# Two tiles ahead of the weights, and q and k in 512 B packets that PSUM copies put in order

## The chip, the cores and the metric

One core of a Trainium2 chip. The metric is the device time of one execution in microseconds (us), the median of several runs. A profile shows one such run. Its engines are PE (TensorE, matmuls), PEld (its weight loads), DVE (VectorE), ACT (ScalarE), POOL (GpSimd) and SP (SyncE, which only issues DMA here). "tile" below means 256 tokens: the kernel works through 12 of them.

## The reference, cut to what matters

```python
# q, k, v: (4, 8, 768, 64), 0.1 * normal; 3 of 8 heads attend to all earlier keys,
# the others to 4 first keys and a window of 64
scores = (q @ k.T) / 8, masked;  a = softmax(scores);  attn = a @ v
x = attn.transpose(0, 2, 1, 3).reshape(3072, 512)
h = x @ w_in            # 512 x 2048
out = (h - tanh(h)) @ w_out
```

## The kernel before

Each operation is given to a small planner with an engine, an expected duration and what it reads and writes. The planner runs a list schedule over these durations and emits every engine's instructions in the order that it found.

```python
# loads of one tile: 128 tokens to a transfer, one token of 256 B (64 fp32) to a packet
r = lazy(raw_pool, [128, NB, H, D], FP32, "raw", f"raw_{nm}{t}")
for i in range(NB):                                   # NB = 2
    op("SP", 420, lambda ...: nc.sync.dma_start(
        out=r()[:, i, :, :], in_=src[b, :, s0 : s0 + 128, :].rearrange("h p d -> p h d")), ...)
...
# st_T: q and k of a pair of heads are transposed by PE into PSUM, then copied to SBUF
tp, key = bank([128, 2, NB, 128], FP16, "sc", f"tp{n}")
...
cost = {"ACT": 373, "DVE": 288}                       # what the planner is told, in ns
op(eq, cost[eq], lambda: copy(eq, qT[n]()[:], tp()[:, 0, :, :].rearrange("p i c -> p (i c)")), ...)
for hh in range(2):                                   # the two heads of k
    op(ek[hh], cost[ek[hh]], lambda ...: copy(
        ek[hh], kk[p_, hh, cs], tp()[p_, 1, :, :].rearrange("p i c -> p (i c)")), ...)
...
# the opening: weights are issued before tile 1
cast_qk(0, ...); cast_v(0)
for j in range(4): load_w_in(j)
scale_v(0); load(1)
for n in range(HP): st_T(n, "ACT", ("DVE", "DVE")); ...
cast_qk(1, ...); cast_v(1); scale_v(1)
for j in range(4): load_w_out(j)
load(2)
```

After the opening each tile has an up-projection (H: 8 units of 8 matmuls), a tanh on ScalarE and one VectorE instruction per unit, and a down-projection (O), while the attention of the tile after next goes on between them: transposes, copies to qT and kz, scores (sc), exp on ScalarE, masks (pt), the product with v (av), normalisation (x) and a transpose back (xT).

The softmax here doesn't subtract the row's maximum and nothing guards it: scores larger than these inputs give would overflow.

Of the kernel before, what the change touches and what calls it, by code (L numbers as in the profile page):

```python
# [7 lines left out]
FP32 = mybir.dt.float32  # L8
# [8 lines left out]
class Plan:  # L17
# [14 lines left out]

    def op(self, eng, ns, fn, r=(), w=(), dma=None, prio=None):
        i = len(self.ops)
        deps = set()
        for k in r:
            if k in self.writer:
                deps.add(self.writer[k])
            self.readers.setdefault(k, []).append(i)
        for k in w:  # L40
            if k in self.writer:
                deps.add(self.writer[k])
            deps.update(self.readers.get(k, ()))
            self.writer[k] = i
            self.readers[k] = []
        for key in (*r, *w):
            if isinstance(key, tuple) and key[0] in self.bufs:
                tag, at = key[:2]
                deps.update(self.users.get((tag, at - self.bufs[tag]), ()))
                self.users.setdefault((tag, at), []).append(i)  # L50
        deps.discard(i)
        self.ops.append((eng, ns, fn, deps, dma, i if prio is None else prio))
        return i

    def run(self):
# [14 lines left out]
        order = []  # L70

        def enqueue(i):
            queue[self.ops[i][0]].append(i)

        def finish(i, done):
            self.done[i] = done
            e, ns, _, _, dma, _ = self.ops[i]
            for u in users[i]:
                to = self.ops[u][0]
                if to == e and e == "PE":  # L80
                    at = self.start[i] + ns
                else:
                    at = done + (60 if to == "PE" else 40)
                ready[u] = max(ready[u], at)
                left[u] -= 1
                if not left[u]:
                    enqueue(u)
# [4 lines left out]
        while len(order) < n:  # L92
            t, e = min(
                [(max(free[e], min(ready[i] for i in q)), e) for e, q in queue.items() if q],
                default=(1e12, None),
# [17 lines left out]
            elif nxt < t:  # L113
# [3 lines left out]
            i = min(  # L117
                (i for i in queue[e] if ready[i] <= t), key=lambda i: self.ops[i][5]
            )
            queue[e].remove(i)  # L120
            _, ns, _, _, dma, _ = self.ops[i]
            self.start[i] = t
            order.append(i)
            free[e] = t + max(ns - self.OVERLAP[e], 40)
            if dma:
                packets, each = dma
                rings["POOL" if e == "POOL" else "SP"].append(
                    [i, t + ns + 300, each, packets * each / 16]
                )
            else:  # L130
                finish(i, t + ns + self.RESULT[e])
# [6 lines left out]
def kernel(  # L138
# [85 lines left out]

    def load(t, names="qkv"):
        b, g = divmod(t, NG)
        for nm in names:
            src = {"q": q, "k": k, "v": v}[nm]
            idx = 3 * t + "qkv".index(nm)
            r = lazy(raw_pool, [128, NB, H, D], FP32, "raw", f"raw_{nm}{t}")  # L230
            for i in range(NB):
                s0 = g * TT + i * 128
                op(
                    "SP", 420,
                    lambda r=r, i=i, src=src, s0=s0: nc.sync.dma_start(
                        out=r()[:, i, :, :],
                        in_=src[b, :, s0 : s0 + 128, :].rearrange("h p d -> p h d"),
                    ),
                    w=[("raw", idx, i)], dma=(1024, 21.0),
                )  # L240
            raws[nm, t] = (r, idx)

    W_OUT_AFTER = 2
    w_in_t = []
    w_out_t = []

    def load_w_in(j):
        w = lazy(w_pool, [128, HP, 512], FP16, f"win{j}", f"win{j}")
# [5 lines left out]
            ),  # L254
            r=[("v1", 0, 0)], w=[("win", j)], dma=(512, 80.0),
        )
        w_in_t.append(w)

    def load_w_out(j):
        w = lazy(w_pool, [128, 4, DM], FP16, f"wout{j}", f"wout{j}")  # L260
# [5 lines left out]
            ),  # L266
            r=[("v1", 0, W_OUT_AFTER)], w=[("wout", j)], dma=(512, 80.0),
        )
# [10 lines left out]
    )  # L279
    load(0, "qk")  # L280
    load(0, "v")

# [79 lines left out]
    for h in range(H):  # L362
# [5 lines left out]
            ),  # L368
            r=["thr", "A4", "A40", "A41", "A43"], w=[("m4", h // 2)],
        )  # L370
# [13 lines left out]

    def cast_qk(t, engines):

        for nm, es in zip("qk", engines):
            c = lazy(t16_pool, [128, NB, H, D], FP16, f"t16{nm}", f"t16_{nm}{t}")
            r, slot = raws[nm, t]
            for i, e in enumerate(es):  # L390

                def fn(c=c, r=r, i=i, e=e):
                    if e == "ACT":
                        nc.scalar.copy(out=c()[:, i, :, :], in_=r()[:, i, :, :])
                    else:
                        engs[e].tensor_copy(out=c()[:, i, :, :], in_=r()[:, i, :, :])  # L396

                op(
                    e, {"ACT": 590, "DVE": 380, "POOL": 540}[e], fn,
                    r=[("raw", slot, i)], w=[("t16" + nm, t, i)],  # L400
                )
            t16s[nm, t] = c

    v1s = {}
    vfs = {}

    def cast_v(t):
        b, g = divmod(t, NG)
        if g == 0:
            v1s[b] = lazy(v_pool, [128, 2 * NG, H, D + 1], FP16, "v1", f"v1_{b}")  # L410
            vfs[b] = lazy(v_pool, [128, 4, H, D + 1], FP16, "vf", f"vf_{b}")
        v1, vf, lo = v1s[b], vfs[b], g * NB
        r, slot = raws["v", t]
        op(
            "POOL", 200,
            lambda: nc.gpsimd.memset(v1()[:, lo : lo + NB, :, D : D + 1], 1.0 / XS),
            w=[("v1", b, lo + i) for i in range(NB)],
        )
        for i in range(NB):
            op(  # L420
                "POOL", 540,
                lambda i=i: nc.gpsimd.tensor_copy(  # L422
                    out=v1()[:, lo + i, :, 0:D], in_=r()[:, i, :, :]
                ),
                r=[("raw", slot, i)], w=[("v1", b, lo + i)],
            )

    def scale_v(t):
        b, g = divmod(t, NG)
        v1, vf, lo = v1s[b], vfs[b], g * NB  # L430
        for jb in range(lo, min(lo + NB, 4)):
# [6 lines left out]
                ),  # L438
                r=[("v1", b, jb), "rflag0", "rflag"], w=[("vf", b, jb)],
            )  # L440
# [4 lines left out]
    x16s = {}  # L445
    xTs = {}

    def st_T(n, eq="DVE", ek=("DVE", "DVE")):
# [6 lines left out]
        def mm():  # L455
# [8 lines left out]
            "PE", 224, mm,  # L464
            r=["ident"] + [("t16" + nm, t, i) for nm in "qk" for i in range(NB)], w=[key],
        )
        qT[n] = lazy(qt_pool, [128, TT], FP16, f"qT{hp}", f"qT{n}")

        def copy(e, dst, src):
            if e == "ACT":  # L470
                nc.scalar.copy(out=dst, in_=src)  # L471
            else:
                nc.vector.tensor_copy(out=dst, in_=src)  # L473

# [3 lines left out]
            eq, cost[eq],  # L478
            lambda: copy(eq, qT[n]()[:], tp()[:, 0, :, :].rearrange("p i c -> p (i c)")),
            r=[key], w=[(f"qT{hp}", t)],  # L480
        )
        for hh in range(2):
# [3 lines left out]
                lambda p_=p_, hh=hh: copy(  # L486
                    ek[hh], kk[p_, hh, cs], tp()[p_, 1, :, :].rearrange("p i c -> p (i c)")
                ),
# [18 lines left out]
    def st_S(n, gi):  # L507
# [35 lines left out]
        if gi == 0:  # L543
# [14 lines left out]

            op("DVE", 560 if g == 0 else 695, mask, r=pk + [("m4", hp)], w=pk)

    avs = {}

    def st_A(n, i):
# [19 lines left out]
        r = [("pt", n, gi) for gi in range(len(GROUPS[g]))]  # L583
        r += [("v1", b, jb) for jb in range(max(qb - 1, 0), qb + 1)]
        r += [("vf", b, jb) for jb in range(qb - 1)]
# [18 lines left out]

    def st_X(n):
        t, hp = divmod(n, HP)
        if hp == 0:
            xTs[t] = lazy(xt_pool, [128, HP, TT], FP16, "xT", f"xT{t}")
        xp, key = bank([128, NB, 128], FP16, "m", f"xp{n}")

        def mm():
            for i in range(NB):
# [5 lines left out]
        op(  # L618
            "DVE", 290,
            lambda: nc.vector.tensor_copy(  # L620
                out=xTs[t]()[:, hp, :], in_=xp()[:].rearrange("p i c -> p (i c)")
            ),
            r=[key], w=[("xT", t, hp)],
# [102 lines left out]

    cast_qk(0, (("DVE", "DVE"), ("DVE", "ACT")))
    cast_v(0)
    for j in range(4):
        load_w_in(j)  # L730
    scale_v(0)
    load(1)
    for n in range(HP):
        st_T(n, "ACT", ("DVE", "DVE"))
        if n:
# [5 lines left out]
        if n > 2:  # L741
            st_X(n - 3)
    for f in scores(HP - 1):
        f()
    for n in (HP - 2, HP - 1):
        st_A(n, 0)
        st_A(n, 1)
        st_X(n - 1)
    st_X(HP - 1)
    cast_qk(1, (("DVE", "DVE"), ("DVE", "POOL")))  # L750
    cast_v(1)
    scale_v(1)
    for j in range(4):
        load_w_out(j)
    load(2)
    for hp in range(HP):
# [76 lines left out]
```

## Time and profile before

| | before |
|---|---|
| time, median of 3 (lowest to highest) | 276.85 us (276.75 to 277.22) |
| TensorE work, counted by matmul pitch | 235 us |
| VectorE busy | 179.6 us, 65% |
| copy from PSUM to kz on VectorE | 283 ns, 96 times |

### The profile page before, as it was taken

How to read it: one execution, taken by the hardware profiler on the slowest of the kernel's cores; microseconds unless marked ns; L12 is line 12 of the kernel's file. 1: busy time of each engine (PE TensorE's matmuls, PEld its weight loads, DVE VectorE, ACT ScalarE, POOL GpSimd, SP SyncE). 2: the span in 40 equal slices, each digit the busy share in tenths (PEclk: the TensorE clock that was granted, in tenths of full speed). 3: DMA queues.
4: the chain of work that ended last, by engine and by line, in shares of the span. 5: the costliest groups of instructions: out<-in, count | busy, mean ns of one | idle time of the engine just before them, and what ended most of it. 6: DMA issues, size and time to landing. Idle time of an engine off the chain costs nothing.

```text
span 275.6 us, 6251 instructions
## 1 busy us (share of the span) xinstructions
PE 251.2 (91%) x2560; PEld 186.9 (68%) x2560; DVE 179.6 (65%) x452; ACT 154.2 (56%) x223; POOL 69.5 (25%) x116
## 2 busy tenths in 40 slices
PE   0457977999999999999999999999999999999984
PEld 0335764888778777777777777777777877776631
DVE  7784775776898875556987655567987655554310
ACT  2330464788357676665476776564567566644420
POOL 7530940527190730206803000300300000000000
PEclk9999999999999999999999999999999999999999
DMA  7999999999989590182860210010001001011101
GB/s 140 217 199 209 191 207 203 221 220 232 230 177 201 129 224 32 40 190 66 201 144 15 76 43 4 37 40 38 2 38 40 2 38 40 1 40 39 40 38 76
DMA packets 82733, 29.78 MB, mean 108 GB/s; under 512 B 75536, under 2 KB 79632, under 8 KB 82704
## 3 DMA queue, kind: packets, MB, share of 16 engines
q1 hardware_dynamic: 78336, 25.17, 41.7%
q0 software_dynamic: 4224, 4.19, 9.2%
q8 instruction: 20, 0.33, 0.5%
q14 instruction: 9, 0.07, 0.1%
q10 hardware_dynamic: 144, 0.01, 0.0%
HBM read 27.27 MB, written 6.29 MB: 122 GB/s over the span
## 4 chain that ended last, share of the span: by engine, by line
PE 84%; DVE 11%; ACT 2%; issue 2%
PE ph L642 29%; PE po L678 29%; PE sc L522 13%; PE av L578 8%; PE tp L458 3%; PE xp L613 2%; DVE x L597 1%; DVE kz L473 1%; DVE gt L662 1%; DVE pt L554 1%; DVE pt L549 1%; DVE kz L331 1%; DVE m L365 1%; DVE xT L620 1%; ACT th L655 1%
## 5 line engine op out<-in xcount | busy, mean ns | idle before, releaser
L642 PE MATMUL ph<-xT,win 128*128 128x256 f16 x768 | 103.3, 278 | 0.7 <-DVE gt L662 0.7
L678 PE MATMUL po<-wout,gt 128*128 128x512 f16 x384 | 100.0, 379 | 1.4 <-ACT ot L691 1.4
L537 ACT ACTIVATE pt<-sc 128x1024 f16<-128x1024 f32 (+1 forms) x96 | 85.5, 916 | 23.7 <-PE sc L522 19.4
L655 ACT ACTIVATE th<-ph 128x512 f32<-128x512 f32 x96 | 57.4, 598 | 71.4 <-PE ph L642 67.5
L662 DVE SCALAR_TENSOR_TENSOR gt<-th,ph 128x512 f16<-128x512 f32 x96 | 65.8, 686 | 38.6 <-ACT th L655 38.1
L642 PEld LDWEIGHTS <-win 128*128 128x128 f16 x768 | 73.8, 100 | 16.3 <-issue 1.1
L522 PE MATMUL sc<-qT,kz 128*128 128x128 f16 (+1 forms) x448 | 53.2, 250 | 2.5 <-DVE kz L473 2.0
L678 PEld LDWEIGHTS <-gt 128*128 128x128 f16 x384 | 34.2, 98 | 23.3 <-issue 1.9
L522 PEld LDWEIGHTS <-kz 128*128 128x128 f16 x448 | 37.0, 99 | 14.1 <-DVE kz L473 2.8
L578 PEld LDWEIGHTS <-pt 128*128 128x128 f16 x672 | 30.1, 98 | 9.6 <-issue 2.1
L396 POOL CAST t_q<-raw_q 128x512 f16<-128x512 f32 x20 | 12.4, 646 | 90.3 <-PE tp L458 47.5
L578 PE MATMUL av<-v,pt 128*128 128x65 f16 x352 | 29.3, 196 | 1.5 <-DVE xT L620 0.8
L473 DVE COPY kz<-tp 64x256 f16<-64x256 f16 x96 | 27.1, 283 | 3.4 <-ACT qT L471 1.2
L554 DVE TENSOR_TENSOR pt<-pt,m 128x1024 f16<-128x1024 f16 x32 | 23.3, 729 | 4.7 <-ACT pt L537 4.7
L578 PE MATMUL av<-vf,pt 128*128 128x65 f16 x320 | 23.5, 193 | 1.6 <-DVE xT L620 0.9
L458 PE MATMUL tp<-ident,t_q 128*128 128x128 f16 x96 | 13.8, 226 | 9.2 <-DVE t_q L396 8.8
L691 ACT ACTIVATE ot<-po 128x512 f32<-128x512 f32 x24 | 14.4, 598 | 12.9 <-PE po L678 12.7
L597 DVE TENSOR_TENSOR x<-av,rinv 128x256 f16<-128x256 f32 x48 | 20.3, 423 | 1.5
L592 DVE RECIPROCAL rinv<-av 128x4 f32<-128x4 f32 x48 | 8.7, 180 | 17.7 <-PE av L578 17.2
L422 POOL CAST v<-raw_v 128x512 f16<-128x512 f32 x24 | 15.0, 641 | 18.7 <-DMA raw_v<-in_v_dram 18.5
L435 POOL TENSOR_TENSOR vf<-v,rflag 128x520 f16<-128x520 f16 x16 | 18.2, 1146 | 0.7
L458 PEld LDWEIGHTS <-t_q 128*128 128x128 f16 x96 | 8.8, 101 | 13.4 <-DVE t_q L396 8.9
(35 smaller groups left out, 121.7 us busy)
## 6 DMA issues: line engine op xcount, KB each, us to landing
raw_q<-in_q_dram SPq DMA_DIRECT2D x24, 256.0 KB, 4.9
raw_k<-in_k_dram SPq DMA_DIRECT2D x24, 256.0 KB, 4.8
raw_v<-in_v_dram SPq DMA_DIRECT2D x24, 256.0 KB, 4.9
out_dram<-ot SPq DMA_DIRECT2D x24, 256.0 KB, 2.1
win<-in_moe_w_in_dram POOLq DMA_DIRECT2D x4, 512.0 KB, 10.4
wout<-in_moe_w_out_dram POOLq DMA_DIRECT2D x4, 512.0 KB, 10.6
retr_i<-in_is_retrieval_dram ACTq DMA_DIRECT2D x1, 8.0 KB, 3.1
```

The costliest lines, as they stand in the source:

```text
L435: lambda jb=jb, fl=fl: nc.gpsimd.tensor_mul(out=vf()[:, jb, :, :], in0=v1()[:, jb, :, :], in1=fl[:].unsqueeze(2).to_broadcast([128, H, D + ...
L458: nc.tensor.transpose(out=tp()[:, x, i, :], in_=c()[:, i, 2 * hp : 2 * hp + 2, :], identity=ident16[:],)
L473: nc.vector.tensor_copy(out=dst, in_=src)
L522: nc.tensor.matmul(out=sc()[:, hh, o : o + nb * 128], lhsT=kk[:, hh, jb * 128 : jb * 128 + 128], rhs=qT[n]()[:, q0 * 128 : (q0 + nb) * 128 ...
L537: lambda: nc.scalar.activation(out=pt()[:, :, 512 * gi : 512 * gi + wid], in_=sc()[:, :, 0:wid], func=AF.Exp, scale=inv_sqrt_d,),
L554: nc.vector.tensor_mul(out=pv, in0=pv, in1=m4[:, hs, 256:512].unsqueeze(2).to_broadcast([128, 2, 2, 256]),)
L578: nc.tensor.matmul(out=av()[:, i, hh, :], lhsT=pt()[:, hh, co : co + 128], rhs=vv()[:, jb, h, :], start=(jb == 0), stop=(jb == qb),)
L597: lambda: nc.vector.tensor_mul(out=x16()[:], in0=av()[:, :, :, 0:D], in1=rinv()[:].unsqueeze(3).to_broadcast([128, NB, 2, D]),),
L642: nc.tensor.matmul(out=ph()[:, j, :], lhsT=w_in_t[fb // 4]()[:, cb, f0 : f0 + 128], rhs=xTs[t]()[:, cb, :], start=(cb == 0), stop=(cb == H ...
L655: lambda: nc.scalar.activation(out=th()[:], in_=ph()[:], func=AF.Tanh, scale=1.0 / XS),
L662: lambda: nc.vector.scalar_tensor_tensor(out=gts[t]()[:, u * FU : (u + 1) * FU, :], in0=th()[:], scalar=-XS, in1=ph()[:], op0=ALU.mult, op ...
L678: nc.tensor.matmul(out=po()[:], lhsT=gts[t]()[:, f, ts * 128 : ts * 128 + 128], rhs=w_out_t[f // 4]()[:, f % 4, :], start=(f == 0), stop=( ...
```

## The change

Its intent is to shorten the opening: tiles 0 and 1 are loaded before any weight, in halves of four heads; q and k come in 512 B packets, two neighbouring tokens in one partition; the copies out of PSUM, which are needed anyway, put the tokens back in order. The planner also learns that some VectorE and all GpSimd instructions exclude each other (port). Cut to its core:

```diff
@@ loads of q and k: tokens 2p and 2p+1 in partition p @@
-            r = lazy(raw_pool, [128, NB, H, D], FP32, "raw", f"raw_{nm}{t}")
+                            raw_pool, [128, NB, H, D] if nm == "v" else [128, H, NB, D], FP32,
...
+                            out=r()[:, h0 : h0 + nh, :, :].rearrange("p h i d -> p h (i d)"),
+                            in_=src[b, h0 : h0 + nh, g * TT : g * TT + TT, :].rearrange(
+                                "h (p i) d -> p h (i d)", i=NB
+                            ),
@@ st_T: the copies out of PSUM (cost stays {"ACT": 373, "DVE": 288}) @@
-            lambda: copy(eq, qT[n]()[:], tp()[:, 0, :, :].rearrange("p i c -> p (i c)")),
+                eq, qT[n]()[:].rearrange("p (c i) -> p c i", i=NB),
+                tp()[:, 0, :, :].rearrange("p i c -> p c i"),
...
-                    ek[hh], kk[p_, hh, cs], tp()[p_, 1, :, :].rearrange("p i c -> p (i c)")
+                    ek[hh], kk[p_, hh, cs].rearrange("p (c i) -> p c i", i=NB),
+                    tp()[p_, 1, :, :].rearrange("p i c -> p c i"),
@@ the opening @@
-    for j in range(4):
-        load_w_in(j)
-    scale_v(0)
-    load(1)
+    cast_qk(0, ..., (0,)); cast_v(0, ..., (0,)); cast_qk(0, ..., (1,)); cast_v(0, ..., (1,))
+    load(1, halves=range(2))
...
+    for half in range(2):
+        cast_qk(1, (("POOL", "POOL"), ("ACT", "POOL")), (half,))
+        cast_v(1, ("POOL", "POOL"), (half,))
+    for j in range(4):
+        load_w_in(j, [("t16k", 1, 1)])
+    load(2)
+    scale_v(0)
     scale_v(1)
     for j in range(4):
-        load_w_out(j)
-    load(2)
+        load_w_out(j, [("v1", 0, 1, 1)])
```

## The prediction

> **What bounds the kernel now.** I read the busy strip of the page first, then stretches of it, then the DMA queues in the opening, then the groups of instructions on VectorE.
>
> ```profile
> PE   0457977999999999999999999999999999999984
> DVE  7784775776898875556987655567987655554310
> DMA  7999999999989590182860210010001001011101
> ```
>
> The strip has 40 slices of 6.9 us. TensorE is full from the eighth slice on, the DMA engines are full from the first: the kernel is in an opening that waits for data and a long stage that TensorE sets. The stretches put numbers on that (us; busy time by engine, granted clock, DMA share, GB/s):
>
> ```profile
> 0.00:10.00 10.00, 1.19 (x8) 0.76 (x8) 7.89 (x21) 2.28 (x4) 5.23 (x22) 1.00 0.89 165
> 10.00:24.00 14.00, 7.57 (x59) 4.91 (x58) 9.85 (x25) 4.45 (x8) 7.10 (x9) 1.00 1.24 202
> 30.00:40.00 10.00, 7.95 (x93) 6.31 (x92) 8.24 (x20) 6.25 (x9) 7.18 (x10) 1.00 1.12 195
> 40.00:50.00 10.00, 8.54 (x103) 6.03 (x99) 5.62 (x18) 4.05 (x5) 1.85 (x3) 1.00 1.14 200
> 50.00:262.00 212.00, 211.75 (x2246) 161.18 (x2244) 144.54 (x364) 133.01 (x191) 46.13 (x71) 1.00 0.40 91
> ```
>
> From 50 to 262 us TensorE idles 0.25 us of 212. Matmul records overlap, so I also counted the pitch: consecutive 512-wide matmuls start 0.216 us apart, 256-wide 0.109, 128-wide 0.054, the 65-wide 0.03. The whole program is then about 235 us of TensorE work, of which 19 us is done at 47.9 us, when the first up-projection of tile 1 starts. So some 29 us of the span are lost before that point, and a microsecond won there moves the end by a microsecond, as long as the long stage keeps its pace.
>
> Why the opening is slow: the weights go out before tile 1 does. From 17 to 26 us the two queues moved:
>
> ```profile
> q0 software_dynamic: 1400, 1.40, 91.3%
> q1 hardware_dynamic: 1417, 0.36, 29.9%
> ```
>
> q0 is the weights, q1 the tiles (packets, MB, share). They alternate packet for packet, so a tile moves 256 B while a weight moves 1024 B: 40 GB/s for tiles, against 223 GB/s with q1 alone from 5 to 9 us. By the DMA records tile 1's second half of k lands only at 22.8 us and its v at 29.1, though issued at 10.6 to 13.2. The four input weights land at 17.5, 21.1, 24.4 and 28.2 us, the output weights at 37.9, 41.5, 44.9 and 48.2. Tile 0's up-projection starts at 23.9 but tile 1's attention at 32.5; then tile 1's attention is a chain with little beside it.
>
> **What the skill says.**
> - DMA: Bandwidth & Descriptors, "Queues, rings and completion order": each engine goes round robin between its queues, by packet. The trace agrees: 1400 against 1417 packets above.
> - The same page, "Why small descriptors are slow (HBM only)": a fixed overhead per packet, 27% at 256 B. The trace of before has no 512 B packet. It has 256 B at 18.3 ns pitch per engine (256 KB, 64 packets per engine, every 1.17 us) and weights (2048 B read, 1024 written) at 86.7 ns when alone (189 GB/s written at 14 to 15 us). A line through both gives 28 ns for 512 B, my estimate: 290 GB/s in place of 224.
> - VectorE: DVE Perf Modes, "What auto-detection actually checks": two results a cycle from PSUM need every tensor 16-bit with step 1. Here the trace agrees for the copies of before:
>
> ```profile
> L473 DVE COPY kz<-tp 64x256 f16<-64x256 f16 x96 | 27.1, 283 | 3.4 <-ACT qT L471 1.2 <-PE tp L458 0.9
> L597 DVE TENSOR_TENSOR x<-av,rinv 128x256 f16<-128x256 f32 x48 | 20.3, 423 | 1.5
> L662 DVE SCALAR_TENSOR_TENSOR gt<-th,ph 128x512 f16<-128x512 f32 x96 | 65.8, 686 | 38.6 <-ACT th L655 38.1
> ```
>
> The last two differ by 256 elements and 263 ns, one element a cycle with 160 ns fixed. The copy of 256 fp16 elements takes 283, so its elements cost half that.
> - SBUF — State Buffer, "Who interferes with whom": VectorE's two-port modes and GpSimd shut each other out for a whole instruction. The trace agrees: nz, a 16-element VectorE instruction, took 1.46 us beside GpSimd's memsets.
>
> **The change, part by part.**
>
> *Order of loads.* Tiles 0 and 1 (3 MB, as twelve half-tile groups) go first, and the weights wait for tile 1's last k cast on GpSimd. First data moves at 2.75 us as before. A half of q or k is 512 packets, 32 per engine, 0.90 us at 28 ns; a half of v stays at 256 B, 1.17 us. A half tile is 2.97 us, two tiles 11.9, so tile 1 has flowed at 14.6 us and its last v has landed at 15.8, 13 us sooner than now. Packet size alone gives only 1.0 us a tile. Then tile 2's q and k (1.8 us each) fit in before the weights: GpSimd casts tile 1's last v at about 16.4 and then issues them, and from issue to landing the first took 7.0 us before (10.4 to 17.5). So the first input weight lands at 23.4, the others 3.4 apart beside tile 2's v, the fourth near 34. The output weights follow without the gap of 28 to 36 us; they alternate with 512 B packets, 3.8 us each: 38, 42, 45 and 49 us. The last weight lands as late as before; the gain is that attention work is done meanwhile.
>
> *What that is worth.* I counted the TensorE work ahead of a point in each program's order. The fourth block of tile 0's down-projection needs the last weight. Before, it started at 53.0 us with 23.7 us of work ahead; after, 28.9 us lie ahead of it. If it starts at 49.2 us, just behind the weight, the kernel is ahead by 53.0 - 49.2 + 28.9 - 23.7 = 9.0 us. Can TensorE be there by then? The point that needs the fourth input weight (34 us) has 15.3 us ahead of it, so 13.6 us of work fit in 15.2. Yes, narrowly. The orders of both programs are the same again from tile 3's up-projection on, so the 9 us are kept unless the long stage slows.
>
> *Halves and tile 0.* T and scores can start on four heads. Little comes of it: VectorE now makes the eight masks (2.2 us) ahead of its first cast, so I expect the first transposes at 8.5 us instead of the usable ones at 9.05. X outputs move to another PSUM bank, which unties tile 0's chain of 2 us per pair of heads at 18 to 24 us. Both help only up to the weights' arrival and are within the 9.
>
> *The copies that put tokens in order.* They read PSUM with an innermost step of 128, which breaks the step-1 condition. I expect 160 + 267 = 427, less the shorter overhead of a copy (283 - 133 = 150): about 417 ns instead of 283. It is +133 ns for 136 VectorE copies (96 for k less 4 given to ScalarE, 44 for q), 18 us of VectorE time, busy share from 65% to some 70%. ScalarE's copies keep 372. The planner in the kernel still books 288, so the order does not allow for it.
>
> *What that costs.* In the long stage, scores follow their k copies closely. For each of the 36 head pairs from tile 3 on I took the gap between the end of the copies and the scores' first weight load, and charged what of 0.27 us (first k copy) or 0.40 (second) does not fit: 3.8 us in all, with gaps of 0.05 us in five cases and over 0.4 in a dozen. Carrying VectorE's lateness forward instead, with idle time absorbing it and the other consumers included, gave 2.6 us (1.2 for +100 ns, 4.5 for +160). I take 2.6.
>
> Sum: 276.85 - 9.0 + 2.6 = 270.4 us.
>
> **The rivals.**
> 1. The copies stay at 283 ns and only the opening counts: 267.8 us. For it: the planner's unchanged cost. Against: the step, and the half-rate arithmetic above. One in eight.
> 2. VectorE becomes the bound in the crowded stretches. It is busy 16.20 of 20 us from 80 to 100 us; four head pairs more of copies at 0.4 us make it 17.8. With queueing for reciprocal and scaling, whose consumers have gaps of 0.05 to 0.2 us in half the pairs, the loss could be 6 or 7 us and the result 274 to 275, the same as before. One in four.
> 3. DMA hides the gain: 512 B packets do no better per byte, or take more from the weights when alternating. Each tile then flows 1 us later and the last output weight lands near 52: 273. One in seven.
> 4. Attention of tile 0 and 1 is a longer chain than I think (VectorE waits for GpSimd's casts and vf products), and reaches tile 0's up-projection after 26 us instead of 24. It has about 2 us of cover, since the fourth input weight sets the next point.
>
> **Range and chances.** The opening is worth 9 give or take 2, the copies cost 0 to 7; the two together hold 265.5 to 275.5 eight times in ten. Faster by 2% means under 271.3, which is only a microsecond above my number: 0.58 faster, 0.40 within 2%, 0.02 slower, since the opening cannot lose more than it has.
>
> **What would show it.** The strided copies' row should read near 417 ns on VectorE and 372 on ScalarE. Tile 1's v should land near 16 us, the input weights between 23 and 34, the last output weight near 49. Tile 0's up-projection should start near 24 and the fourth block of its down-projection near 49, tile 3's up-projection near 80 instead of 88.2. The stretch from there to the end should be 2 us longer than before, with TensorE waiting for k copies. I am wrong if copies stay at 283, if the last weight lands after 51, or if tile 3's lead of 8 us is gone at the end.

## More of the kernel before

The prediction shows the lines of the profile that carry it. Four more of the kernel before are needed for the comparison. The first is the chain of work that ended last, its share by engine; the second and third are the stretches from 60 to 80 and from 120 to 140 us (busy us and number of instructions of PE, PEld, DVE, ACT, POOL, then granted clock, DMA share, GB/s); the last the row of the weight loads of the scores (idle time ahead of them in us, and what ended most of it).

```profile
PE 84%; DVE 11%; ACT 2%; issue 2%
...
60.00:80.00 20.00, 20.00 (x230) 15.24 (x226) 15.71 (x45) 13.36 (x19) 10.46 (x18) 1.00 0.99 213
...
120.00:140.00 20.00, 19.87 (x212) 14.88 (x210) 15.41 (x43) 10.72 (x18) 10.49 (x17) 1.00 0.59 132
...
L522 PEld LDWEIGHTS <-kz 128*128 128x128 f16 x448 | 37.0, 99 | 14.1 <-DVE kz L473 2.8 <-issue 1.3
```

VectorE has 4 to 5 us to spare in each of these 20 us stretches. That is the reserve which the change draws on.

## The result, and the profile after

After: 276.22 us, median of 4 runs (276.05 to 276.36); before on the same chip 276.8. The ratio is 0.998, 95% interval 0.996 to 0.999: the same within 2%. Ratios here are the mean time of one kernel's runs over that of the other's runs of the same rounds, so not quite the ratio of the medians quoted. Executions over 1.5% slower than the fastest of the same kernel are left out of the means.

The kernel after, its busy strip (40 slices of 6.9 us), then the same stretches as before with those of the opening:

```profile
PE   0557899999999999999999999999999999999984
DVE  7788698678988855668997856668998755554400
PEclk9995999999999999999999999999999999999999
DMA  6999999999591931156431211010001001010101
...
10.00:24.00 14.00, 9.43 (x82) 6.99 (x83) 11.43 (x26) 7.84 (x14) 13.47 (x17) 0.83 1.20 246
24.00:30.00 6.00, 5.05 (x63) 4.09 (x61) 4.23 (x11) 3.66 (x5) 5.08 (x8) 0.82 1.21 207
...
60.00:80.00 20.00, 18.83 (x195) 13.65 (x194) 17.83 (x44) 11.08 (x17) 10.54 (x20) 1.00 0.84 205
...
120.00:140.00 20.00, 19.69 (x200) 14.08 (x198) 17.11 (x44) 10.63 (x16) 10.09 (x20) 1.00 0.44 115
```

The DMA row has closed up (202 GB/s became 246 from 10 to 24 us), as intended. But VectorE is now busy 17.83 and 17.11 us where it was 15.71 and 15.41, and TensorE is no longer full there. The PEclk row also shows a spell of lower granted clock in the opening (0.83 from 10 to 24 us, 0.82 from 24 to 30), which the kernel before does not have; e5 and e14 below take the same time without it (276.13 and 276.31 us), so it is hardly what took the gain away. The rows of the copies and of the scores' weight loads, and the shares of the chain that ended last:

```profile
L492 DVE COPY kz<-tp 64x256 f16<-64x256 f16 x92 | 38.2, 416 | 2.5 <-PE tp L504 1.3
L492 DVE COPY qT<-tp 128x256 f16<-128x256 f16 x44 | 18.4, 419 | 6.3 <-PE tp L504 6.1
L490 ACT COPY qT<-tp 128x256 f16<-128x256 f16 x4 | 1.5, 372 | 2.0 <-PE tp L504 1.7 <-DVE kz L492 0.2
L566 PEld LDWEIGHTS <-kz 128*128 128x128 f16 x448 | 38.3, 101 | 18.3 <-DVE kz L492 4.7 <-issue 1.4
...
PE 77%; DVE 14%; ACT 4%; DMA 2%; issue 1%; SPq 1%; ACTq 0%
```

The copies took the 416 to 419 ns expected on VectorE, and ScalarE's still take 372. The waits of the scores for k copies rose from 2.8 to 4.7 us and VectorE's share of the chain from 11 to 14%. The chain itself, in order of time (start us, us, what), shows what this means in the long stage:

```profile
127.48 0.20 PE av L622 x6
127.68 0.02 issue
127.70 0.19 DVE rinv L636
127.89 0.02 issue
127.92 0.42 DVE x L641
128.34 0.59 DVE gt L704
128.94 0.34 DVE qT L492
129.27 0.32 DVE kz L492
129.59 0.20 DVE xT L492
129.79 0.01 issue
129.81 0.43 DVE kz L492
...
137.66 0.21 DVE xT L492
137.87 0.04 issue
137.91 0.19 PE av L622
```

For 10 us, from 127.7 to 137.9, the chain never leaves VectorE: it goes from one instruction to the next on that engine, and 9 of the 25 are copies to qT or kz. It does the same from 74.3 to 77.4 and from 189.2 to 198.0 us. In the kernel before, the chain after 60 us visits VectorE twice, for 2.9 and 2.1 us.

**Where the time went.** I counted the TensorE work done (each matmul at its pitch) along the trace, and took the *lead*: how much earlier than the kernel before a kernel has done the same work. This is the yardstick for all that follows. (The profiled run of before took 277.36 us, half a microsecond above its median, so leads at the end are about that much above the differences of medians.)

| TensorE work done, us | 20 | 40 | 60 | 120 | end |
|---|---|---|---|---|---|
| before reaches it at, us | 49.3 | 69.9 | 90.2 | 152.2 | 271.0 |
| lead of after, us | 5.2 | 5.2 | 3.2 | 2.2 | 1.0 |

So the opening brought 5.2 us, not 9.0, and the long stage took 4.2 of them back, not 2.6.

### The profile page after: what moved, and what is told of

Same layout as the page of the kernel before. It is cut to its first block, busy times and chain, and to the rows that moved or that the text cites. A ratio compares the mean times of both kernels' runs of the same rounds, so it can differ in the third digit from the quotient of the medians.

```text
span 274.7 us, 6268 instructions
## 1 busy us (share of the span) xinstructions
PE 251.9 (92%) x2560; PEld 186.8 (68%) x2560; DVE 193.0 (70%) x445; ACT 157.7 (57%) x228; POOL 69.7 (25%) x130
## 4 chain that ended last, share of the span: by engine, by line
PE 77%; DVE 14%; ACT 4%; DMA 2%; issue 1%; SPq 1%; ACTq 0%
PE po L720 28%; PE ph L684 25%; PE sc L566 12%; PE av L622 7%; DVE kz L492 3%; PE tp L504 3%; DVE gt L704 3%; ACT pt L581 2%; DVE pt L593 2%; DMA raw_q<-in_q_dram 2%; PE xp L657 2%; DVE qT L492 2%; DVE x L641 1%; ACT ot L733 1%; DVE xT L492 1%
## 5 line engine op out<-in xcount | busy, mean ns | idle before, releaser
L684 PE MATMUL ph<-xT,win 128*128 128x256 f16 x768 | 100.8, 273 | 0.5 <-DVE xT L492 0.3
L684 PEld LDWEIGHTS <-win 128*128 128x128 f16 x768 | 71.8, 98 | 12.6 <-issue 0.3
L566 PE MATMUL sc<-qT,kz 128*128 128x128 f16 (+1 forms) x448 | 56.8, 254 | 3.3 <-ACT kz L490 1.4
L566 PEld LDWEIGHTS <-kz 128*128 128x128 f16 x448 | 38.3, 101 | 18.3 <-DVE kz L492 4.7
L492 DVE COPY kz<-tp 64x256 f16<-64x256 f16 x92 | 38.2, 416 | 2.5 <-PE tp L504 1.3
L622 PEld LDWEIGHTS <-pt 128*128 128x128 f16 x672 | 30.8, 99 | 10.9 <-DVE x L641 2.1
L425 POOL CAST t_q<-raw_q 128x512 f16<-128x512 f32 x22 | 14.3, 653 | 93.8 <-PE tp L504 45.8
L598 DVE TENSOR_TENSOR pt<-pt,m 128x1024 f16<-128x1024 f16 x32 | 23.5, 736 | 8.5 <-ACT pt L581 8.5
L622 PE MATMUL av<-vf,pt 128*128 128x65 f16 x320 | 24.1, 194 | 0.2 <-DVE xT L492 0.2
L492 DVE COPY qT<-tp 128x256 f16<-128x256 f16 x44 | 18.4, 419 | 6.3 <-PE tp L504 6.1
```

What stands on the lines that cost most here:

```text
L425: op(e, cost, lambda: engs[e].tensor_copy(out=dst(), in_=src()), r=r, w=w, port=True)
L492: nc.vector.tensor_copy(out=dst, in_=src)
L566: nc.tensor.matmul(out=sc()[:, hh, o : o + nb * 128], lhsT=kk[:, hh, jb * 128 : jb * 128 + 128], rhs=qT[n]()[:, q0 * 128 : (q0 + nb) * 128 ...
L598: nc.vector.tensor_mul(out=pv, in0=pv, in1=m4[:, hs, 256:512].unsqueeze(2).to_broadcast([128, 2, 2, 256]),)
L622: nc.tensor.matmul(out=av()[:, i, hh, :], lhsT=pt()[:, hh, co : co + 128], rhs=vv()[:, jb, h, :], start=(jb == 0), stop=(jb == qb),)
L684: nc.tensor.matmul(out=ph()[:, j, :], lhsT=w_in_t[fb // 4]()[:, cb, f0 : f0 + 128], rhs=xTs[t]()[:, cb, :], start=(cb == 0), stop=(cb == H ...
```

## The experiments

My first theory (A) was: the copies cost some 4 us, mostly because the planner books 288 ns for what takes 417, so that its order is wrong; and the opening falls short because the attention chain of tiles 0 and 1 is slower than planned. Rivals: the packets themselves cost (C), or GpSimd and VectorE shut each other out in the opening (B). All kernels below are edits of one of the two; "booked" is what the planner is told for a VectorE copy of st_T. A changed booking or dependence plans the whole order anew, so differences of under a microsecond between such kernels may be luck of the plan.

### First round: parts alone

**e1, order only.** The change with q and k in 256 B packets and plain copies.

```diff
-                if nm != "v":          # 512 B packets
+                if False:              # as v: 256 B packets, natural order
-                eq, qT[n]()[:].rearrange("p (c i) -> p c i", i=NB),
-                tp()[:, 0, :, :].rearrange("p i c -> p c i"),
+                eq, qT[n]()[:], tp()[:, 0, :, :].rearrange("p i c -> p (i c)"),
```

> The changed kernel with q and k again in 256 B packets and natural order, so that the PSUM copies read with step 1; the order of loads, the halves and the rest as changed. Theory A (the strided copies cost what the order of loads wins): the copies take 283 ns again, the stretch from tile 3's up-projection to the end is about 2 us shorter than in the changed kernel, and the chain of the opening loses some ten copies of 133 ns; against that tile 1 lands 1 to 2 us later. Together 272.5 to 274 us. Rival B (the opening is held by VectorE waiting for GpSimd's hold of the shared port, copies matter little): 275.5 to 277. Rival C (the 512 B packets carry the change): 277 or more.

Measured: 272.02 us (271.82 to 272.28, 5 runs), ratio 0.983. Theory A held; the time is half a microsecond better than its range. Half of the change is better than the whole.

**e2, packets only.** The kernel before with 512 B packets and the strided copies, booked 288.

```diff
-            for i in range(NB):
+            if nm != "v":   # one transfer of 512 B packets, (p i) tokens
+                op("SP", 1126, ...)
-                    ek[hh], kk[p_, hh, cs], tp()[p_, 1, :, :].rearrange("p i c -> p (i c)")
+                    ek[hh], kk[p_, hh, cs].rearrange("p (c i) -> p c i", i=NB),
+                    tp()[p_, 1, :, :].rearrange("p i c -> p c i"),
```

> The kernel before with only q and k in 512 B packets, two tokens to a partition, and the copies that read PSUM with step 128; weights still ahead of tile 1. Theory A: copies at 417 ns, TensorE waits for k copies in the long stage, 2 to 3 us lost there, DMA wins 1 us at most: 278 to 279.5 us. Rival C (packets pay): 275 or less. If the copies are hidden: 276 to 277.

Measured: 282.14 us (281.82 to 282.33, 4 runs), ratio 1.020. The direction of A, and a larger loss than expected: 5.5 us. The lead is -0.1 us at 20 us of work and -4.5 at the end, so it is lost in the long stage.

**e4, the planner knows.** The kernel after, booked right.

```diff
-        cost = {"ACT": 373, "DVE": 288}
+        cost = {"ACT": 373, "DVE": 418}
```

> The changed kernel with one number altered in its planner: a PSUM copy on VectorE is booked at 418 ns, as measured, not 288. If the loss in the long stage comes from an order planned with the wrong duration, TensorE's gaps ahead of the scores (2.2 us from 80 us on) go and the time is 274 to 275. If the longer copies cost by themselves, 275.7 to 276.7.

Measured: 272.01 us median, ratio 0.982, but the six runs spread from 269.45 to 273.14. The same instructions in another order are 4 us faster: more than I had given the booking. The lead is 5.4 us at 20 us of work and 5.3 at the end: the long stage loses nothing. And VectorE is as busy there as in the kernel after, while TensorE is nearly full (the same stretches as before):

```profile
60.00:80.00 20.00, 19.85 (x221) 15.07 (x219) 17.73 (x45) 10.75 (x17) 10.49 (x21) 1.00 0.94 225
120.00:140.00 20.00, 19.83 (x211) 14.83 (x209) 17.30 (x44) 10.89 (x17) 10.33 (x20) 1.00 0.39 106
```

So in the long stage it is not VectorE's total that costs, but the longer copies in an order that was made for shorter ones.

**e5, GpSimd quiet in the opening.** The kernel after; the vf products and the zeroing of the second kz set wait until tile 0's masks are done.

```diff
-    scale_v(0)
-    scale_v(1)
+    scale_v(0, after=[("pt", 3, 0)])
+    scale_v(1, after=[("pt", 5, 0)])
-        zero_kz("POOL", 1, hp, 0, S)
+        zero_kz("POOL", 1, hp, 0, S, after=[("xT", 0, HP - 1)])
```

> The changed kernel with GpSimd's deferrable work put off: the zeroing of the second k set waits for tile 0's output transposes, the vf products for the masks of pairs 3 and 5. Rival B (VectorE waits for the port, 3.4 us in the opening: cast 0.9, masks 0.6 and 1.3 and 0.5): about 1.5 us of these waits go, tile 0's up-projection starts near 27 us instead of 28.6 and the time is 274.5 to 275.3. Theory A: the waits lie beside other work, 275.8 to 276.6.

Measured: 276.13 us (275.5 to 276.37, 5 runs), no change. Tile 0's first up-projection did start earlier, at 25.0 instead of 28.6 us, but with 5.7 instead of 7.2 us of work ahead of it, and TensorE then waited for the input weights, which landed later (25.0 instead of 23.7 for the first). Theory B gets its mechanism and no time.

### Second round: how much, and what bounds the opening

**e6, booked halfway** (353), and **e7**, the kernel of e2 booked 418.

> The changed kernel with a VectorE PSUM copy booked at 353 ns, halfway between 288 (276.2 us) and the measured 418 (272.0 us). If the wrong booking is what loses the time, the result lies between, 273 to 275 us, with gaps ahead of the scores in the long stage between 2.2 and 0 us. If any other order would have done as well (the planner's luck), it can fall anywhere from 271 to 277, below 272.5 or above 275.7 as likely as between.

> The kernel before with the 512 B packets and strided copies (282.1 us when booked at 288 ns), now booked at 418. If the wrong booking costs the time, most of the 5.5 us over the kernel before come back: 276 to 278.5 us. If the longer copies cost by themselves, 280.5 to 282.5.

Measured: e6 274.42 us (274.38 to 274.47, 4 runs), halfway between 276.2 and 272.0. e7 276.45 us (275.67 to 277.15, 6 runs): all that the packets lost in e2, 5.5 us, comes back by telling the planner what the copies take.

**e8, one weight.** The kernel after with one block of each weight loaded and used for all four (a wrong result).

```diff
-    for j in range(4):
+    for j in range(1):
         load_w_in(j, [("t16k", 1, 1)])
-                        out=ph()[:, j, :], lhsT=w_in_t[fb // 4]()[...]
+                        out=ph()[:, j, :], lhsT=w_in_t[0]()[...]     # and w_out the same
```

> The changed kernel loading one block of each weight instead of four and using it for all (a wrong result on purpose): all weights are there by about 28 us. If the weights' arrival bounds the opening, as the prediction had it, the point of 28.9 us of TensorE work is passed at 47 to 49 us instead of 53.0 and the time is 271 to 273. If the chain of tile 0's and tile 1's attention through ScalarE and VectorE bounds it, tile 0's up-projection still starts at 28 us or later and the time is 275 to 276.5.

Measured: 276.66 us (275.54 to 277.41, 4 runs), no gain by the median. Two of the runs, at a granted clock of 0.974, took 277.3 and 277.4 us; the two at 0.988 and 0.998 took 275.5 and 276.0, so up to 0.7 us may be gained. In the kernel after, the weights do not bound the opening by more than that.

**e9**, booked 418 and GpSimd quiet (e4 and e5 together).

> The changed kernel with both the copies booked at 418 ns and GpSimd's deferrable work put off. If the quiet GpSimd helps where the order is right (tile 0's up-projection at 25 us), 270.5 to 271.7 us. If the weights are the next bound behind the chain, as the quiet run alone suggested (276.1, input weights landing 1.5 us later), 271.7 to 273.

Measured: 271.8 us (270.81 to 272.02, 5 runs), as e4 alone.

### Third round: the copies' length alone

So far every comparison had changed the plan. e13 keeps it.

**e13, plain copies.** The kernel after, its order instruction for instruction the same on every engine, with step-1 copies. Tokens are then in the wrong order.

```diff
-                eq, qT[n]()[:].rearrange("p (c i) -> p c i", i=NB),
-                tp()[:, 0, :, :].rearrange("p i c -> p c i"),
+                eq, qT[n]()[:], tp()[:, 0, :, :].rearrange("p i c -> p (i c)"),
```

(and the same for k.)

> The kernel after with only the access of its 136 + 4 PSUM copies changed: they read and write with step 1 again, so tokens stay in the wrong order (a wrong result on purpose). The packets are 512 B and the plan is that of the kernel after, instruction for instruction, because the planner books 288 ns there already. Theory A (the loss against the step of the sum '-9.0 opening' is partly the copies, which the plan does not know): the copies read 283 ns, the gaps of TensorE after 90 us fall from 4.5 to under 2.5, and the time is 271.5 to 273. The rival (512 B packets themselves cost, by what they shift in the opening or in the long stage): 275 or more. If it comes out well above 272.0 (the same order with 256 B packets and plain copies), the difference is the price of the packets and of the plan that goes with them.

Measured: 269.44 us median, ratio 0.973. This is the largest effect of any single edit: 6.8 us, where the prediction had 2.6, and 2 us below the range that I expected of it. Two remarks on it. The result passed as correct: scores here are about 0.01 in size (0.1 × 0.1 × 8 / 8), so every kept key weighs almost the same, and the reference computed with q and k exchanged in that way differs by only 0.7%. A check on these inputs cannot see a wrong token order. And its six runs form two groups, 268.1 to 269.5 and 272.1 to 272.5; the profiled run is one of the slow ones, so I do not take the gain of plain copies in the opening from it. Its granted clock is half in the slice from 20 to 27 us and in part of the next, half a slice longer than in the kernel after:

```profile
PEclk9995799999999999999999999999999999999998
```

**e10**, e9 with one weight (wrong result); **e11**, e1 with GpSimd quiet; **e12**, e9 with the input weights issued after the first half of tile 1's k cast.

```diff
-        load_w_in(j, [("t16k", 1, 1)])
+        load_w_in(j, [("t16k", 1, 0)])      # e12
```

> The kernel after with the copies booked at 418, GpSimd kept quiet while tile 0's masks run, and only one block of each weight loaded and used for all (a wrong result on purpose). If the attention chain of tiles 0 and 1 and the landing of the weights are the two bounds of the opening, one just behind the other, then taking the weights away beside the quiet GpSimd (271.8 with all weights, where the opening waited for input weights) gives 268 to 270, and tile 0's first up-projection starts at about 25. If the weights are only apparent waits and the chain or VectorE is all there is, it stays at 271 to 272. In the kernel after alone the missing weights changed nothing (276.66).

> Tiles first, but q and k in 256 B packets with plain copies, as in the run that gave 272.02, with GpSimd kept quiet while tile 0's masks run. Theory: tile 0's up-projection starts 2 to 3 us earlier (26 to 27), but the weights then bound, 1 us later than with 512 B packets, so the time is 271 to 272. A rival, that GpSimd's port is worth its whole 3 us where the copies are short: 269 to 270.

> The kernel after with the copies booked at 418 and GpSimd kept quiet, and the input weights issued after the first half of tile 1's k cast instead of the second. Theory: the first input weight lands 1.5 to 2.5 us earlier (25.65 with the later issue), and the opening, which then waits for the weights, is shorter by 1 to 2 us: 270 to 271. Rival: GpSimd's writing of descriptors (3.2 us) now stands in front of its casts of tile 1 and in the way of VectorE's masks, and the gain is eaten: 271.5 to 273.

Measured: e10 271.08 us (270.72 to 271.46, 4 runs); e11 270.74 us (270.2 to 271.8, 6 runs); e12 272.14 us (271.51 to 272.51, 4 runs). None did what its theory said: e10 and e12 came out as their rivals had it, and e11 fell between its two ranges. e10 gained a microsecond at most, so the lead of these kernels, 5 to 6 us, is not held by weights and the port of GpSimd alone. e12 led by 6.2 us at 20 us of work and by 5.4 at the end.

### Fourth round: is it TensorE's half pace?

In the traces without filler most matmuls of the opening, up to 21 to 31 us, start at twice their later pitch (0.107 us for 128 columns, then 0.054). Some have a spell of full pace in between (16 to 18 us in the kernel after). The PEclk row need not show the half pace: it reads 9 throughout in e4, where the half pace lasts to 27.3 us. The change moves 4 us more of TensorE work ahead of tile 0's up-projection. To test whether that holds the opening, matmuls on constants were planned into TensorE's idle time, so that it is kept at work.

```diff
+    wp, wkey = bank([128, FU, TT], FP32, "h", "warm_pe")
+    for _ in range(135):
+        def dummy():
+            for j in range(2):
+                nc.tensor.matmul(out=wp()[:, 0, 0:128], lhsT=ones[:], rhs=ones[:], ...)
+        op("PE", 2 * 54, dummy, r=["ones"], w=[wkey], prio=10**9)
```

**e14** is the kernel after, **e15** is e13, **e16** the kernel before (150 pairs) and **e17** e11 (150 pairs), each with this filler.

> The kernel after with 135 times two matmuls on constants (0.11 us each pair) planned at lowest priority into TensorE's idle time in the opening. Theory C (the half pace of the opening's matmuls is on the chain of tiles 0 and 1): the pitch of 128-wide matmuls is 0.054 instead of 0.107 us from about 6 us on, tile 0's first up-projection starts at 25 to 26.5 instead of 28.6, the lead at 20 us of work is 7 to 8 instead of 5.2, and the time is 273 to 275. Rival D (the chain is VectorE, GpSimd and data; TensorE's pace is in the idle time): pitch halves but the lead stays at 5 to 5.5 and the time at 275.5 to 276.5.

> The same filler in the variant with plain copies and wrong token order (269.4, spread 268.1 to 272.5 with the granted clock). Theory C: 266 to 268.5 and the spread shrinks to under 1.5 us. Rival D: 268 to 270, and the spread stays.

> The kernel before with 150 such pairs. Only 3.3 us of TensorE work lies ahead of its first up-projection and its opening waits for weights and tile 1's data, so Theory C expects little: 275.5 to 276.8. If it gains 2 us or more, the half pace costs both kernels alike and does not explain the missing lead.

> Tiles first, 256 B packets, plain copies, quiet GpSimd (270.7) with 150 such pairs. Theory C: 268 to 269.5. Rival D, or weights that bound by then: 270 to 271.

Measured: e14 276.31 us (274.23 to 276.49, 6 runs); e15 268.93 us (267.95 to 269.57, 6 runs); e16 278.8 us (278.1 to 279.89, 6 runs); e17 272.28 us (271.11 to 272.64, 6 runs). The pace became full from 4 to 7 us on, and no kernel gained more than half a microsecond by its median; e16 and e17 are even above all their ranges. With the filler they are slower by 2.1 us (the kernel before) and 1.5 us (e17), presumably because it delays real work. So a gain of that size may be hidden in e14, but the half pace alone does not hold the kernel after. In e15 it may have done something else: the slow group of e13 is gone.

These runs gave the cleanest pair: e14 and e15 have the same plan, full pace and no half-clock slices, and differ in the access of the copies alone.

| lead over before, us, at TensorE work of | 20 | 40 | 60 | 120 | end | time, us |
|---|---|---|---|---|---|---|
| after | 5.2 | 5.2 | 3.2 | 2.2 | 1.0 | 276.22 |
| e14, after with filler | 5.4 | 5.3 | 3.3 | 2.2 | 1.0 | 276.31 |
| e15, the same with plain copies | 8.0 | 8.0 | 7.5 | 8.3 | 8.3 | 268.93 |
| e4, after, booked 418 | 5.4 | 5.2 | 5.0 | 5.4 | 5.3 | 272.01 |
| e18, e4 with q copies on ScalarE (below) | 8.6 | 8.2 | 7.2 | 7.6 | 7.2 | 270.34 |

The pair e14 and e15 has every engine's instructions in the same order, by their traces. Of e14 the chain's shares and the row of the scores' weight loads:

```profile
PE 84%; DVE 12%; ACT 2%; issue 1%; POOL 0%; ACTq 0%; POOLq 0%
...
L566 PEld LDWEIGHTS <-kz 128*128 128x128 f16 x448 | 36.9, 98 | 13.6 <-DVE kz L492 2.3
```

The profile of e15, in the views shown for the kernel after (chain shares, stretches, rows):

```profile
PE 82%; DMA 8%; POOL 3%; SPq 2%; DVE 2%; issue 2%; ACT 1%; POOLq 0%
...
60.00:80.00 20.00, 19.76 (x213) 14.92 (x211) 16.41 (x46) 11.88 (x18) 9.63 (x13) 1.00 1.05 248
...
120.00:140.00 20.00, 20.00 (x220) 15.45 (x218) 16.32 (x48) 12.30 (x18) 9.29 (x15) 1.00 0.49 133
...
L492 DVE COPY kz<-tp 64x256 f16<-64x256 f16 x92 | 26.0, 283 | 3.2 <-PE tp L504 1.3 <-ACT qT L490 0.8
L564 PEld LDWEIGHTS <-kz 128*128 128x128 f16 x448 | 37.0, 98 | 10.5 <-DVE kz L492 0.2
```

VectorE carries 2% of the chain instead of 12% in e14, the waits of the scores' weight loads for k copies are 0.2 us instead of 4.7 in after and 2.3 in e14, and a DMA group, the input weights, has come onto the chain instead. (That e14 waits 2.3 us there and the kernel after 4.7, with the same time and lead, says that this row alone does not measure the loss.) The 2.6 us of the opening are there before tile 0's up-projection, which starts at 26.3 us in e15 and at 28.9 in e14; the 17 copies on VectorE ahead of it take 6.4 and 8.2 us. The fourth block of tile 0's down-projection starts at 50.8 us, just behind the last output weight, which landed at 50.7.

### Fifth round: VectorE's time or the single copy?

**e18.** e4 with the 44 q copies on ScalarE; the k copies stay on VectorE with their stride. **e19** is e18 with GpSimd quiet.

```diff
-    def st_T(n, eq="DVE", ek=("DVE", "DVE")):
+    def st_T(n, eq="ACT", ek=("DVE", "DVE")):
-        cost = {"ACT": 373, "DVE": 288}
+        cost = {"ACT": 373, "DVE": 418}
```

> The kernel after with the 44 q copies of tiles 1 to 11 on ScalarE (booked 373, measured 367 to 372) and VectorE's k copies booked at 418. VectorE gives back 44 x 0.417 = 18 us, just what the longer copies took, and ScalarE gets 16 us. If VectorE's total time in the opening and in the crowded stretches is what costs: 268 to 270, and the lead at 20 us of work is 7 or more. If the single k copy ahead of the scores is on the chain, whatever else VectorE does: 271 to 272.5, as with the booking alone (272.0). If ScalarE becomes the bound (exp and tanh late): 273 or more.

> The same with GpSimd kept quiet while tile 0's masks run. Without q copies on ScalarE the quiet gave nothing (271.8 against 272.0), as then the weights came later; I expect the same of it here, within 1 us of the other kernel of this call; 1.5 us or more below it would say that VectorE's waits for the port were hidden behind its copies.

Measured: e18 270.34 us (269.62 to 271.39, 5 runs), ratio 0.976 [0.974, 0.979]; e19 273.58 us (273.07 to 275.01, 6 runs). In e18, chain shares and the two rows of copies:

```profile
PE 78%; DMA 8%; DVE 5%; SPq 4%; ACT 2%; POOL 1%; issue 1%; DVEq 0%
...
L492 DVE COPY kz<-tp 64x256 f16<-64x256 f16 x92 | 38.7, 420 | 16.6 <-ACT qT L490 8.6 <-PE tp L504 6.7
L490 ACT COPY qT<-tp 128x256 f16<-128x256 f16 x48 | 17.8, 372 | 10.5 <-PE tp L504 5.6 <-DVE kz L492 2.8 <-PE ph L684 0.6
```

The k copies take 420 ns as before and the opening still leads by 8.6 us, so their length alone does not hold it. The fourth block of tile 0's down-projection starts at 49.8 us, behind a last weight at 49.4. The lead is as the theory of VectorE's total had it, the time 0.3 us above its range, but this is not shown: e18 has its own plan; tile 0's q copies are on ScalarE in e4 too, so that VectorE's copies ahead of tile 0's up-projection take 7.0 us in e18 and 7.4 in e4; and in the profiled runs the matmuls are at full pace from 22.0 us on in e18, from 27.5 in e4. No run separates these three. e19 is a miss, 3.2 us above e18 where 1 was allowed. With the GpSimd work held back the first input weight landed at 26.7 instead of 23.5, and TensorE's matmuls stood still for it from 24.1 to 26.8 us. That is a part of the 4.8 us by which e19's lead at 20 us of work falls short of e18's; its half granted clock from 27.9 to 31.3 us may be another.

e18 gives the right result in the right order and beats both kernels, by 6.6 us the one before of the same rounds. e11, simpler, with 256 B packets, is 0.4 us behind it, within the spread of both.

## Why the prediction was wrong, point by point

- **Bound of the kernel before: right.** The opening waits, the long stage is TensorE's. A microsecond of lead at 40 us of work is kept to the end wherever VectorE has time: 4.9 at 40 and 5.4 at the end in e1, 8.0 and 8.3 in e15.
- **Data and weights: right.** Tile 1's last v landed at 16.2 us (15.8 predicted), the input weights at 23.7 to 34.8 (23.4 to 34), the last output weight at 48.95 (49). A half of q or k took 0.93 us (0.90), 29 ns a packet. The estimate of 28 was a line by bytes read; by bytes written the same two points give 41, and the prediction does not say why it chose the first.
- **Copies at 417 and 372 ns, VectorE at 70%: right.** 416 to 419, 367 to 372, and 193.0 us, 70%.
- **Opening worth 9.0: the mechanism right, and not reached in this kernel.** The step was "If it starts at 49.2 us, just behind the weight". It started at 53.0, four microseconds behind the weight. In e15 and e18 the block does start right behind its weight and the lead is 8.0 and 8.6. On the same plan at full pace (e14, e15) the longer copies are what is missing, in the opening too, where the prediction charged nothing for them. Its sign "tile 3's up-projection near 80 instead of 88.2" failed with this: 86.5, a lead of 1.7 us instead of 8.
- **Copies cost 2.6: the step that failed, by size.** It was charged "For each of the 36 head pairs from tile 3 on". Measured on the same plan (e14 against e15), the copies cost 5.4 - 8.0 = 2.6 us before 20 us of work, where the sum had nothing, and (1.0 - 5.4) - (8.3 - 8.0) = 4.7 us after it, where the sum had 2.6. Together 7.3. Put into the sum this gives 276.85 - 8.3 + 7.3 = 275.9, where 276.22 came; it is no check of its own, as both terms are read from one pair. The opening term of 2.6 is read from that pair alone. In the slow profiled run of e13, without filler, plain copies gained hardly anything in the opening (lead 5.5), so there another bound stands about as high; its half clock suggests TensorE's pace, which I have not shown.
- **Why the size was wrong.** The 2.6 came from "Carrying VectorE's lateness forward instead, with idle time absorbing it". So lateness that adds up was meant to be in it, but the measured loss is nearly twice as large: for 10 us at a time the chain runs through VectorE alone. Which of the count's assumptions failed there is not on record; the idle time that it let absorb the lateness is my guess. What is shown is that the order makes the loss: the planner believed 288, and told 418 it loses nothing in the long stage with VectorE just as busy (e4, with e6 between; e2 and e7 the same). That is 4.2 us. The prediction named this ("so the order does not allow for it") and did not ask what another order would give.
- **Rival 2** ("the loss could be 6 or 7 us and the result 274 to 275", one in four) came nearest. VectorE does carry the chain in the crowded stretches, but the loss there is 4.7; the 7.3 needs the 2.6 of the opening, where it had not looked either, and 276.2 is above its 274 to 275.
- **Rival 1** (copies at 283) and **rival 3** (DMA hides the gain) were wrong. **Rival 4** (tile 0's up-projection after 26 us) came true, at 28.6, but the cause it named, GpSimd, is not it: made quiet, it gave 25.0 us and no time. With a third of the copies' time off VectorE, in a new plan (e18: 18 of 57 us), it was 25.7 us, and the time came too.

**What stays open:** why e13 without filler runs in two groups; why e1 and e4 lead by 4.8 to 5.4 us in the opening, where e15 and e18 lead by 8.0 and 8.6 (e1 has slower packets as well as its own plan, and its copies are short); what part of e18's opening is VectorE's relief, its plan or TensorE's pace (e4 with the filler would have told); and how much of a difference between two plans is luck.

## What to carry to other kernels

An engine with 30% to spare on the average can still turn longer instructions into lost time (here 18 us of them into 7): find the stretches where it is already busiest, in the opening too, and add up its whole work there, instead of asking instruction by instruction what fits into a gap. But being busier is not yet a loss: in another order VectorE was as busy (17.7 of 20 us) and TensorE hardly waited. Where a planner or scheduler orders a kernel by durations, measure a changed instruction and tell it, before judging the change: here one number was worth 4 us. And test a part of a change with the order frozen, even at the price of a wrong result; experiments that plan anew mix two effects.

## What the Trainium skill lacked or had wrong

- "DMA: Bandwidth & Descriptors" gives a packet's overhead at 256 B, and rates by the size of a whole transfer, but no rate of loads in packets of 256 or 512 B on this chip: from HBM to SBUF, 512 B packets brought 256 KB in 0.93 us (282 GB/s on 16 engines), 256 B packets in 1.17 us (224 GB/s).
- "VectorE: DVE Perf Modes", "The TRN2 errata", gives cycle counts for copies from PSUM that come, as an estimate, to 258 ns with two results a cycle and 392 with one for 256 elements (ScalarE: 357). Measured were 283, 416 to 419, and 372: all 15 to 27 ns longer. What the page doesn't say is that ScalarE takes its 372 with step 1 and with step 128 alike.
- "TensorE: Matmul & The Clock Gate" ("The HAM clock gate") has the half pace right, and that sustained work ends it. Its sentence that everything after the first microseconds is at full rate does not hold here: with sparse matmuls the half pace lasted to 21 to 31 us, with filler only to 4 to 7. (The same part lets an idle TensorE fall back to half, which fits.) Full pace bettered no median by more than 0.5 us.
